# A recurrent attention kernel on one core: joint PV halves copied by bank, filler matmuls moved into the waits around Wo, the part copy in one instruction, and layer norm of the x rows one segment earlier

## The chip, the cores and the metric

The kernel runs on one core of one Trainium2 chip. The metric is device time in microseconds (us); a quoted time is the median of several executions. The engines are PE (TensorE), DVE (VectorE), ACT (ScalarE), POOL (GpSimd) and SP, which here only starts DMAs. The granted clock is the share of the full TensorE clock that the profile records as let through.

## The reference, cut to what matters

Part A is a transformer with a recurrent memory. It walks over 64 segments of 32 rows; 8 memory rows of each segment's output are the input of the next, so the segments form a chain. Part B, which follows, is a gated MLP and is not touched by the change.

```python
for s in range(n_seg):                       # 64 segments
    xs = x[:, s * seg_len:(s + 1) * seg_len, :]
    h = jnp.concatenate([mem, xs], axis=1)   # 8 memory rows + 32 rows
    q, k, v = h @ Wq, h @ Wk, h @ Wv         # 32 heads of 128 (written short)
    p = _softmax(jnp.where(mask, q @ k.T * scale, -1e9))
    o = einsum('bhte,hed->btd', p @ v, Wo)
    mem = o[:, :M, :]                        # M = 8: feeds the next segment
    outs.append(o[:, M:, :])
```

## The kernel before

A small emitter records every operation in program order with the tiles that it reads and writes, and derives semaphore waits. Each engine is given its own operations in program order, and in the traces they come in that order (PE from 502.66 to 507.24 us of before: PV, PV, Wo, WoX, mem_out, then the next Q/K). Two engines that read one PSUM bank are made to wait for each other.

The heads are handled in two halves `b` of 16. Names used below: **Q/K** are the 64 matmuls that project a segment (`QK`); **PV** is probabilities times V for one half; **Wo** is the output projection; **part copy** brings its result from PSUM to SBUF; **mem_out** makes the next memory rows of it. Work that no segment waits for is used as filler: **WoX** is the output projection of rows that were set aside, batched over four segments, and **V rows** (`gv`) and Q/K of x rows (`gx`) are projections of a later chunk of x.

```python
# end of a segment, before
ev = gv.pour(VXN[i16])          # V rows: 8 matmuls in most segments, 16 in two of 16, 0 in the last two
ev += gx.pour(16)               # Q/K of x rows, 16 matmuls
PV_half(s, 0)                   # writes columns 0:160 of banks 0, 1, 6, 7
cT_evac(0, 0, "act")            # banks 0 and 1
cT_evac(0, 1, "dve")            # banks 6 and 7
PV_half(s, 1)                   # the same columns again: must wait for the copies
cT_evac(1, 0, "act")
cT_evac(1, 1, "dve")
for f in ev: f()                # copies of finished V rows (ACT) and Q/K rows (DVE)
Wo(0); Wo(1)                    # 32 matmuls into bank OB
cTx_copy(s)
part_evac(s)                    # ACT 256 columns, then DVE 256 columns of the same bank
late = []
if rb > 0: WoX_mm(rb - 1, j4)   # 8 matmuls
if j4 == 2 and 3 <= rb + 2 < RB:
    ln_inplace(0)               # layer norm of 128 x rows: DVE, POOL, DVE
    xT(0, XB)                   # 4 PE transposes of them
    late.append(lambda: ring_copy(rb + 2, XB))
# ... the same with index 1 for i16 == 13 ...
mem_out(s)                      # 16 small matmuls, then ACT writes hT of segment s + 1
for f in late: f()
if rb > 0 and j4 == 3: WoX_evac(rb - 1)           # ACT: PSUM to SBUF
# ... cut ...
if j4 == 3: F_group(rb, XB); F_add(rb, XB)
if j4 == 3 and rb >= 1: WoX_scatter(rb - 1, WXB); h_done(rb - 1, WXB)   # PE, waits for WoX_evac
```

`j4` is the segment's index modulo 4, `i16` modulo 16, and `rb` counts blocks of four segments. The chunks of x rows are used up after 48 segments, so the last 16 segments have neither `gv` nor `gx`.

## Time and profile before

| | before |
|---|---|
| median | 1140.59 us (1138.38 to 1141.48) |
| the 64 segments, of the 1143.7 us span | 56.1 to 926.1 us |
| ordinary segment (start of Q/K to start of the next Q/K) | 12.42 us; 11.97 in the last 16 |
| every fourth segment (j4 = 2) and its follower | 15.05 and 14.8 us |

The page of the profile, lines of the span, of PE's busy time and of the chain that ended last (the last work, followed back step by step to what released it); the row PEclk shows 40 slices of the span, in tenths of the full TensorE clock.

```profile
span 1143.7 us, 41433 instructions
...
PE 947.0 (83%) x18997; PEld 468.6 (41%) x18997; DVE 504.7 (44%) x1123; ACT 483.1 (42%) x1095; POOL 108.0 (9%) x276
...
PEclk8799999999999999999999999989899879999999
...
PE 73%; ACT 12%; DVE 6%; issue 2%; SPq 2%; DMA 2%; POOL 1%; ACTq 0%
```

TensorE is the chain, but not all of it: the rest are waits for copies on ACT and DVE. The next view is the chain in order of time (start us, duration us, engine and line) through the end of an ordinary segment.

```profile
502.73 0.20 PE f_ps L546 x16
...
503.05 0.43 ACT f_cT L565
...
503.52 0.37 PE f_ps L546 x16
...
503.92 1.87 PE f_ps L576 x32
...
505.82 0.39 ACT f_part L587
...
506.23 0.43 DVE f_part L588
...
506.71 0.25 PE f_ps L594 x8
...
506.99 0.20 ACT f_hT L597
...
507.24 3.64 PE f_ps L436 x64
```

PV of half 0 (L546) has to be copied (L565) before half 1 may overwrite the banks, and Wo (L576) starts 1.19 us after the first PV. From Wo's end at 505.79 to the next Q/K (L436) it is 1.45 us: two copies one after the other, then half of mem_out (L594), then a small copy. The two halves of the part copy read one bank; this kernel's emitter makes the second reader wait for the first, and the trace shows it as ACT 0.39 and then DVE 0.43.

The same view at the end of a segment with j4 = 2:

```profile
531.50 0.61 DVE f_st L334
...
532.14 0.19 DVE f_mv L335
...
532.41 0.23 POOL f_rs L336
...
532.72 0.58 POOL f_rs L338
...
533.32 0.42 DVE f_xn L340
...
533.79 0.40 PE f_ps L346 x4
...
534.71 5.33 PE f_ps L436 x64
```

Here layer norm (L334 to L340) is on the chain, because the transposes (L346) wait for it and mem_out stands behind the transposes in PE's order. And the next Q/K take 5.33 us, not 3.64. The view by stretches (stretch, its length, then busy us of PE and so on; the figure 1.00 or 0.68 after POOL is the granted clock) shows why:

```profile
519.66:523.30 3.64, 3.64 (x81) 1.90 (x85) 1.08 (x3) 1.79 (x3) 0.00 (x0) 1.00 0.58 156
534.71:540.04 5.33, 5.33 (x82) 2.37 (x85) 1.08 (x3) 2.12 (x4) 0.00 (x0) 0.68 0.01 3
```

The waits, longest in total first (who <- for whom: us in total, times, longest), have this for the layer norm and for the PV copies:

```profile
PE f_ps L346 <- DVE f_xn L340: 56.6, 20, 5.8
...
PE f_ps L546 <- ACT f_cT L565: 35.1, 64, 0.6
```

### The profile page before, as it was taken

What the parts mean: (1) busy time and instruction counts of PE and PEld (TensorE: products, weight loads), DVE (VectorE), ACT (ScalarE), POOL (GpSimd) and SP (SyncE); (2) the same over time, 40 slices, a digit from 0 to 9 for tenths busy, and PEclk for the clock granted to TensorE, in tenths of its full rate; (3) what the DMA queues carried; (4) which work ended last, traced back from release to release, by engine and by line L of the source; (5) the groups of instructions that cost most, each with busy time, mean ns of one, the idle gap of its engine ahead of it and who ended that gap; (6) DMA issues with size and microseconds to landing.
All of it is one profiled execution on the core that took longest, in us unless ns stands there. A gap on an engine that the chain in (4) does not pass through costs nothing.

```text
span 1143.7 us, 41433 instructions
## 1 busy us (share of the span) xinstructions
PE 947.0 (83%) x18997; PEld 468.6 (41%) x18997; DVE 504.7 (44%) x1123; ACT 483.1 (42%) x1095; POOL 108.0 (9%) x276
## 2 busy tenths in 40 slices
PE   5588888878888888788888888878788857799998
PEld 5344444434444444344444444433333313334443
DVE  2144454444444545454545444444444335544343
ACT  2155544544454545454545454545454423520000
POOL 4000010010000001010001000100101001210000
PEclk8799999999999999999999999989899879999999
DMA  9931111111111212111111120201011036002201
GB/s 343 293 76 41 30 44 31 48 38 37 31 44 30 44 30 54 32 37 31 44 30 50 29 60 17 60 16 50 22 38 42 11 116 230 1 1 83 92 14 34
DMA packets 93492, 67.36 MB, mean 59 GB/s; under 512 B 54392, under 2 KB 78336, under 8 KB 93312
## 3 DMA queue, kind: packets, MB, share of 16 engines
q1 hardware_dynamic: 93312, 64.65, 18.9%
q8 instruction: 151, 2.47, 0.9%
q14 instruction: 29, 0.24, 0.1%
HBM read 39.46 MB, written 16.78 MB: 49 GB/s over the span
## 4 chain that ended last, share of the span: by engine, by line
PE 73%; ACT 12%; DVE 6%; issue 2%; SPq 2%; DMA 2%; POOL 1%; ACTq 0%
PE f_ps L436 22%; PE f_ps L576 11%; PE f_ps L952 9%; PE f_ps L530 7%; PE f_ps L380 5%; PE f_ps L546 3%; PE f_ps L496 3%; DVE f_part L588 2%; ACT f_cT L565 2%; ACT f_E_sb L489 2%; ACT f_part L587 2%; ACT f_R_sb L508 2%; PE f_ps L399 2%; PE f_ps L907 2%; PE f_ps L940 2%
## 5 line engine op out<-in xcount | busy, mean ns | idle before, releaser
L436 PE MATMUL f_ps<-f_arena,f_hT 128*32 128x512 bf16 x4096 | 255.5, 406 | 15.2 <-ACT f_hT L597 15.1
L443 ACT ACTIVATE f_Tst<-f_ps 128x512 bf16<-128x512 f32 x256 | 152.9, 597 | 142.8 <-PE f_ps L436 142.8
L436 PEld LDWEIGHTS f_ps<-f_arena,f_hT 128*32 128x32 bf16 x4096 | 111.3, 102 | 136.2 <-issue 29.3
L530 PE MATMUL f_ps<-f_arena,f_hT 128*32 128x512 bf16 x2048 | 143.6, 378 | 0.0
L576 PE MATMUL f_ps<-f_arena,f_cT 128*32 128x512 bf16 x2048 | 132.0, 403 | 0.0
L449 DVE STREAM_TRANSPOSE f_QT<-f_Tst 128x256 uint32<-128x256 uint32 x128 | 56.5, 442 | 156.7 <-ACT f_Tst L443 156.7
L952 PE MATMUL f_ps<-f_arena 128*128 128x512 bf16 x448 | 99.3, 379 | 3.0 <-DVE f_arena L957 2.4
L567 DVE TENSOR_SCALAR f_cT<-f_ps 128x320 bf16<-128x320 f32 x128 | 63.0, 492 | 70.6 <-PE f_ps L552 70.6
L565 ACT ACTIVATE f_cT<-f_ps 128x320 bf16<-128x320 f32 x128 | 56.0, 437 | 79.9 <-PE f_ps L552 79.9
L452 DVE STREAM_TRANSPOSE f_KT<-f_Tst 128x256 uint32<-128x256 uint32 x128 | 57.0, 445 | 63.4 <-ACT f_Tst L443 63.4
L346 PE MATMUL f_ps<-f_ident,f_xn 128*128 128x128 bf16 x144 | 16.1, 243 | 80.9 <-DVE f_xn L340 56.6
L546 PE MATMUL f_ps<-f_E_sb,f_V_sb 32*128 32x40 bf16 x2048 | 43.8, 179 | 46.9 <-ACT f_cT L565 35.1
L459 POOL COPY f_QT<-f_arena 128x256 bf16<-128x256 bf16 x64 | 29.9, 467 | 438.8 <-PE f_ps L481 438.7
L576 PEld LDWEIGHTS f_ps<-f_arena,f_cT 128*32 128x32 bf16 x2048 | 50.8, 100 | 50.1 <-issue 8.7
L380 PE MATMUL f_ps<-f_hTe,f_arena 128*128 128x128 bf16 x1024 | 69.6, 226 | 0.0
L380 PEld LDWEIGHTS f_ps<-f_hTe,f_arena 128*128 128x128 bf16 x1024 | 61.1, 102 | 20.4 <-issue 20.4
L588 DVE CAST f_part<-f_ps 128x256 bf16<-128x256 f32 x64 | 27.2, 425 | 91.6 <-ACT f_part L587 91.6
L952 PEld LDWEIGHTS f_ps<-f_arena 128*128 128x128 bf16 x448 | 43.5, 98 | 56.5 <-DVE f_arena L957 3.8
L516 DVE SCALAR_TENSOR_TENSOR f_E_sb<-f_R_sb,f_E_sb 128x160 bf16<-128x160 f32 x128 | 41.7, 326 | 54.6 <-ACT f_R_sb L512 54.6
L587 ACT ACTIVATE f_part<-f_ps 128x256 bf16<-128x256 f32 x64 | 24.6, 384 | 88.1 <-PE f_ps L576 88.1
L546 PEld LDWEIGHTS f_ps<-f_E_sb,f_V_sb 32*128 32x128 bf16 x2048 | 28.8, 91 | 68.9 <-ACT f_cT L565 42.3
L489 ACT ACTIVATE f_E_sb<-f_ps,f_shift 128x224 bf16<-128x224 f32 x128 | 56.9, 445 | 0.0
(96 smaller groups left out, 1171.5 us busy)
## 6 DMA issues: line engine op xcount, KB each, us to landing
wT_d<-f_wst SPq DMA_DIRECT2D x32, 256.0 KB, 2.3
f_arena<-wT_d SPq DMA_DIRECT2D x32, 256.0 KB, 5.8
f_arena<-in_A_Wq_dram SPq DMA_DIRECT2D x4, 1024.0 KB, 8.7
f_arena<-in_A_Wk_dram SPq DMA_DIRECT2D x4, 1024.0 KB, 13.6
f_arena<-in_A_Wv_dram SPq DMA_DIRECT2D x4, 1024.0 KB, 11.6
f_arena<-in_A_Wo_dram SPq DMA_DIRECT2D x4, 1024.0 KB, 13.8
vext_d<-f_Vs SPq DMA_DIRECT2D x32, 128.0 KB, 2.0
f_Vx<-vext_d SPq DMA_DIRECT2D x64, 64.0 KB, 2.5
```

What stands on the lines that cost most here:

```text
L380: pe(lambda e, h=h, dc=dc, hh=hh: e.matmul(ps[:, bank, hh * 128:(hh + 1) * 128], lhsT=ws[:, dc, h * DH:(h + 1) * DH], rhs=hTe[:, ck % 2, d ...
L436: pe(lambda e, dc=dc, c=c, rhs=rhs: e.matmul(ps[32 * c:32 * c + 32, bank, :], lhsT=hT[:, sl, dc, :], rhs=rhs, start=(dc == 0), stop=(dc == ...
L443: act(lambda e: e.activation(out=Tst[:, tb, :].rearrange("p (hp i r) -> p hp i r", i=32, r=2), in_=ps[:, bank, :].rearrange("p (hp r i) -> ...
L449: dve(lambda e: e.transpose(out=dst, in_=src), reads=[("T", tb)], writes=[("QT", b)])
L452: dve(lambda e: e.transpose(out=dst, in_=src), reads=[("T", tb)], writes=[("KT", b)])
L489: act(lambda e: e.activation(out=E_sb[:, b, :], in_=ps[:, bank, 0:224], func=ACT.Exp, scale=scale, bias=shift_sb[:, 0:1]), reads=[PB(bank) ...
L530: pe(lambda e, dc=dc, c=c, c0=c0: e.matmul(ps[32 * c:32 * c + 32, bank, :], lhsT=hT[:, sl, dc, :], rhs=w_v[:, dc, c0:c0 + 512], start=(dc ...
L546: pe(lambda e, q=q, c=c, g=g: e.matmul(ps[:, PVB[c], g * 40:(g + 1) * 40], lhsT=V_sb[q, b, g * 128:(g + 1) * 128], rhs=E_sb[q, b, g * 40:( ...
L565: act(lambda e: e.activation(out=dst, in_=src, func=ACT.Copy, scale=UNSC), reads=[PB(b0), PB(b0 + 1)], writes=[("cT", b, part_)])
L567: dve(lambda e: e.tensor_scalar(out=dst, in0=src, scalar1=UNSC, scalar2=None, op0=ALU.mult), reads=[PB(b0), PB(b0 + 1)], writes=[("cT", b, ...
L576: pe(lambda e, h=h, c=c: e.matmul(ps[32 * c:32 * c + 32, OB, :], lhsT=cTh[:, h, 8:40], rhs=w_o[:, h, :], start=(h < 4), stop=(h >= H - 4), ...
L952: pe(lambda e, fb=fb, sc=sc, bank=bank, tb=tb: e.matmul(ps[:, bank, 0:TB], lhsT=z2[:, sc, fb * 128:(fb + 1) * 128], rhs=wTb[tb % 2][:, :, ...
```

## The change

Four things at once. (1) PV's two halves write different columns of the banks, so they run together, and each copy takes one bank with both halves in it; Wo takes the heads bank by bank. (2) WoX moves into the wait for these copies, and the V rows move from in front of PV into the wait for the part copy. (3) The part copy is one ACT instruction. (4) Loads and layer norm of the x rows come one segment before their transposes.

```diff
@@ PV_half: the same banks, other columns for b = 1
-                    ps[:, PVB[c], g * 40:(g + 1) * 40], lhsT=..., rhs=...,
+                    ps[:, PVB[c], c0:c0 + 40], lhsT=..., rhs=...,      # c0 = 160 * b + 40 * g
@@ cT_evac: one bank, both halves
-        src = ps[:, b0:b0 + 2, 0:160]
-        dst = cT[:, b, 2 * part_:2 * part_ + 2, :]
+        src = ps[:, PVB[c], 0:320]
+        dst = cT[:, c, :]
@@ part_evac
-        act(... out=part[:, s % 4, 0:256], in_=ps[:, OB, 0:256] ...)
-        dve(... out=part[:, s % 4, 256:512], in_=ps[:, OB, 256:512] ...)
+        act(... out=part[:, s % 4, :], in_=ps[:, OB, :] ...)
@@ the segment (load_x: j4 == 1 became j4 == 0; load_xe: i16 == 12 became 11)
-        ev = gv.pour(VXN[i16])
-        ev += gx.pour(16)
+        ev = gx.pour(16)
         PV_half(s, 0)
-        cT_evac(0, 0, "act")
-        cT_evac(0, 1, "dve")
         PV_half(s, 1)
-        cT_evac(1, 0, "act")
-        cT_evac(1, 1, "dve")
+        cT_evac(0, "act")
+        cT_evac(2, "dve")
+        cT_evac(1, "act")
+        cT_evac(3, "dve")
         for f in ev:
             f()
-        Wo(0)
-        Wo(1)
+        if rb > 0:
+            WoX_mm(rb - 1, j4)
+        Wo((0, 2), True, False)
+        Wo((1, 3), False, True)
         cTx_copy(s)
         part_evac(s)
-        late = []
-        if rb > 0:
-            WoX_mm(rb - 1, j4)
+        if j4 == 1 and 3 <= rb + 2 < RB:
+            ln_inplace(0)
+        if i16 == 12 and 2 <= ck + 1 < NCK:
+            ln_inplace(1)
+        late = gv.pour(VXN[i16])
         if j4 == 2 and 3 <= rb + 2 < RB:
-            ln_inplace(0)
             xT(0, XB)
... cut: the same for index 1, and the head order of WoX and cTx ...
```

More of the change, by code (lines that the diff above doesn't have):

```diff
@@ L217, in fast_path @@
     R_sb = sb("R_sb", [128, 2, 160], F32)
-    cT = sb("cT", [128, 2, 4, 160], BF)
+    cT = sb("cT", [128, 4, 320], BF)
     part = sb("part", [128, 4, 512], BF)
@@ L545, in PV_half @@
                 q = slice(32 * c, 32 * c + 32)
-                pe(lambda e, q=q, c=c, g=g: e.matmul(
-                    ps[:, PVB[c], g * 40:(g + 1) * 40], lhsT=V_sb[q, b, g * 128:(g + 1) * 128], rhs=E_sb[q, b, g * 40:(g + 1) * 40],
+                c0 = 160 * b + 40 * g
+                pe(lambda e, q=q, c=c, g=g, c0=c0: e.matmul(
+                    ps[:, PVB[c], c0:c0 + 40], lhsT=V_sb[q, b, g * 128:(g + 1) * 128], rhs=E_sb[q, b, g * 40:(g + 1) * 40],
                     start=(g == 0), stop=False, skip_group_check=True, tile_position=(32 * c, 0)),
@@ L552, in PV_half @@
             pe(lambda e, q=q, c=c: e.matmul(
-                ps[:, PVB[c], 0:160].rearrange("p (g q) -> p g q", q=40)[:, :, 0:16], lhsT=Vx[q, xb, b, :],
+                ps[:, PVB[c], 160 * b:160 * b + 160].rearrange("p (g q) -> p g q", q=40)[:, :, 0:16], lhsT=Vx[q, xb, b, :],
                 rhs=E_sb[q, b, 160:224].rearrange("p (g q) -> p g q", q=16),
@@ L558, in fast_path, with cT_evac, Wo @@
     UNSC = 2.0 ** -64
-    def cT_evac(b, part_, eng):
-        b0 = 0 if part_ == 0 else 6
-        src = ps[:, b0:b0 + 2, 0:160]
-        dst = cT[:, b, 2 * part_:2 * part_ + 2, :]
+    def cT_evac(c, eng):
+        src = ps[:, PVB[c], 0:320]
+        dst = cT[:, c, :]
         if eng == "act":
-            act(lambda e: e.activation(out=dst, in_=src, func=ACT.Copy, scale=UNSC), reads=[PB(b0), PB(b0 + 1)], writes=[("cT", b, part_)])
+            act(lambda e: e.activation(out=dst, in_=src, func=ACT.Copy, scale=UNSC), reads=[PB(PVB[c])], writes=[("cT", c)])
         else:
             dve(lambda e: e.tensor_scalar(out=dst, in0=src, scalar1=UNSC, scalar2=None, op0=ALU.mult),
-                reads=[PB(b0), PB(b0 + 1)], writes=[("cT", b, part_)])
-    cTh = cT[:].rearrange("p b c (g q) -> p (b c g) q", q=40)
-    def Wo(b, lo=0, hi=16):
-        for hh in range(lo, hi):
-            h = 16 * b + hh
-            c = h % 4
-            pe(lambda e, h=h, c=c: e.matmul(ps[32 * c:32 * c + 32, OB, :], lhsT=cTh[:, h, 8:40], rhs=w_o[:, h, :],
-                                            start=(h < 4), stop=(h >= H - 4), tile_position=(0, 32 * c)),
-               reads=[("cT", b, hh // 8), ("Wo", h // 8)], writes=[PB(OB)])
+                reads=[PB(PVB[c])], writes=[("cT", c)])
+    cTh = cT[:].rearrange("p c (b g q) -> p (c b g) q", b=2, q=40)
+    def Wo(cs, first, last):
+        for k, c in enumerate(cs):
+            for bg in range(8):
+                b, g = bg // 4, bg % 4
+                h = 16 * b + 4 * c + g
+                i = 8 * c + bg
+                pe(lambda e, h=h, g=g, i=i, k=k, b=b: e.matmul(
+                    ps[32 * g:32 * g + 32, OB, :], lhsT=cTh[:, i, 8:40], rhs=w_o[:, h, :], start=(first and k == 0 and b == 0),
+                    stop=(last and k == len(cs) - 1 and b == 1), tile_position=(0, 32 * g)),
+                    reads=[("cT", c), ("Wo", h // 8)], writes=[PB(OB)])
     def cTx_copy(s):
@@ L582, in cTx_copy @@
         dst = cTx[:, (s // 4) % 2, :, 8 * j:8 * j + 8]
-        pool(lambda e: e.tensor_copy(out=dst, in_=cTh[:, :, 0:8]), reads=[("cT", b, p_) for b in range(2) for p_ in range(2)],
+        pool(lambda e: e.tensor_copy(out=dst, in_=cTh[:, :, 0:8]), reads=[("cT", c) for c in range(4)],
              writes=[("cTx", (s // 4) % 2)])
     def part_evac(s):
-        act(lambda e: e.activation(out=part[:, s % 4, 0:256], in_=ps[:, OB, 0:256], func=ACT.Copy), reads=[PB(OB)], writes=[("part", s % 4, 0)])
-        dve(lambda e: e.tensor_copy(out=part[:, s % 4, 256:512], in_=ps[:, OB, 256:512]), reads=[PB(OB)], writes=[("part", s % 4, 1)])
+        act(lambda e: e.activation(out=part[:, s % 4, :], in_=ps[:, OB, :], func=ACT.Copy), reads=[PB(OB)], writes=[("part", s % 4)])
     def mem_out(s):
@@ L595, in mem_out @@
                                                          rhs=G_sb[:, :], start=True, stop=True, skip_group_check=True, tile_position=(0, 32 * c)),
-                   reads=[("part", s % 4, dc // 2), "G"], writes=[PB(GB)])
+                   reads=[("part", s % 4), "G"], writes=[PB(GB)])
         act(lambda e: e.activation(out=hT[:, slot(s + 1), :, 0:M], in_=ps[:, GB, 0:DC * M].rearrange("p (dc c) -> p dc c", c=M), func=ACT.Copy),
@@ L604, in F_group @@
                                        tile_position=(0, 32 * j)),
-               reads=[("part", j, 0), ("part", j, 1), "F"], writes=[PB(bank)])
+               reads=[("part", j), "F"], writes=[PB(bank)])
     def F_add(rb, bank):
@@ L614, in WoX_mm @@
     def WoX_mm(rb, qr):
-        for hh in range(8):
-            h = 8 * qr + hh
-            c = h % 4
-            pe(lambda e, h=h, c=c: e.matmul(ps[32 * c:32 * c + 32, WXB, :], lhsT=cTx[:, rb % 2, h, :], rhs=w_o[:, h, :],
-                                            start=(h < 4), stop=(h >= H - 4), tile_position=(0, 32 * c)),
+        for bg in range(8):
+            b, g = bg // 4, bg % 4
+            h = 16 * b + 4 * qr + g
+            pe(lambda e, h=h, g=g, i=8 * qr + bg: e.matmul(ps[32 * g:32 * g + 32, WXB, :], lhsT=cTx[:, rb % 2, i, :], rhs=w_o[:, h, :],
+                                                           start=(i < 4), stop=(i >= H - 4), tile_position=(0, 32 * g)),
                reads=[("cTx", rb % 2), ("Wo", h // 8)], writes=[PB(WXB)])
@@ L738, in fast_path @@
             wT_piece(s // 2)
-        if j4 == 1 and 3 <= rb + 2 < RB:
+        if j4 == 0 and 3 <= rb + 2 < RB:
             load_x(rb + 2, 0)
-        if i16 == 12 and 2 <= ck + 1 < NCK:
+        if i16 == 11 and 2 <= ck + 1 < NCK:
             load_xe(ck + 1, 1)
@@ L788, in fast_path @@
         if i16 == 13 and 2 <= ck + 1 < NCK:
-            ln_inplace(1)
             xT(1, XB)
```

## The prediction

> **What bounds it now.** The recurrence over 64 segments takes 870 of the 1143.7 us span (timeline: first segment at 56.1 us, last ends at 926.1); the 217 us after it do not change. Inside a segment TensorE works in program order and is the chain: the chain of waits gives PE 73%, ACT 12%, DVE 6%. Starts of the segments' Q/K matmuls (PE timeline) give 12.42 us for an ordinary segment, 11.97 us in the last 16 (no filler), but 15.05 us for every fourth, followed by 14.8 us.
>
> **The long segments.** There the timeline shows PE idle 2.75 us before the transposes L346: layer norm of the x rows (0.69 + 0.18 on DVE, 0.22 + 0.57 on POOL, 0.41 on DVE, with hops) starts only after DVE's half of the part copy, and the transposes stand ahead of mem_out in PE's order. Excess 15.05 - 12.42 = 2.63 us, 15 times. In 13 of them the next Q/K matmuls then take 5.3 us (once 6.1, once 4.8), not 3.64; the windows view gives a clock of 0.68 there against 1.00. [...]
>
> **Costing of the change** (chain of waits, ordinary segment):
> 1. Layer norm one segment earlier runs while DVE has nothing urgent. Saves 15 x 2.63 = 39 us, less about 0.3 us each because the transposes (0.4 us) now follow the V rows in the part wait: -35 us.
> 2. With that idle gone, the slow Q/K stretches go: 13 x 1.69 = 22, counted as -20 us.
> 3. PV: now PV0, copies 0.43, PV1, first Wo matmul 1.19 us after PV0's start. Together: PV about 0.5, one copy 0.49 of each bank pair, second pair hidden behind Wo's first half; WoX's 0.43 us fills the copy wait. About 1.0 us: 64 x 0.19 = -12 us.
> 4. Part copy: now ACT 0.39, then DVE 0.43 after it, mem_out in two parts, 1.45 us from Wo's end to the next Q/K. One 512-wide ACT copy (0.59, as L406) and all of mem_out: about 1.20. 64 x 0.25 = -16 us.
> 5. V rows (L399, 8 matmuls 0.43 us) leave the stretch before PV, where TensorE was full, for the part wait, where they fit: 36 x 0.43; in 6 segments with 16 of them 0.2 no longer fits: -19 us.
> 6. Added: the V copy on ACT (0.59) now stands ahead of WoX_evac in the 8 segments where both occur, and the scatter waits for it: +5 us.
> 7. The last 16 segments have six Wo at 3.56 us instead of 1.87 (slow clock). WoX in the copy wait thickens that stretch: perhaps -3 us.
>
> Sum about -100 us; nearly all is on the chain. I take 1044 us, 80% range 1028 to 1064. Faster by over 2%: 0.96; within 2%: 0.03; slower: 0.01.
>
> **What would show it.** Idle before L346 from layer norm falls from 56.6 us to the start-up's part; Q/K at 3.64 us throughout; PE waits "L546 <- ACT cT" (35 us) vanish; segments near 11.5 us, every fourth about 0.4 to 0.9 longer; Wo's end to Q/K about 1.2 us; scatter waits (9 us) grow by about 5.
>
> **What would make it wrong.** The clock: the wait positions move, the last 16 segments lose WoX from their part wait, and new slow stretches of 1.7 us each could appear, or all vanish (10 us more). The switch between row-tiled PV and column-tiled WoX might cost, or Wo might wait for the DVE copy longer than thought. Layer norm on DVE could delay the next Q transpose.

The sum: -35 - 20 - 12 - 16 - 19 + 5 - 3 = -100 us. The 1.69 us of item 2 is what the trace of before shows, 5.33 - 3.64 us.

## The result, and the profile after

| | before | after |
|---|---|---|
| median | 1140.59 us | 1034.06 us (1033.13 to 1034.27) |
| ratio | | 0.9067 (0.9051 to 0.9083) |
| profiled span, mean clock | 1143.7 us, 0.954 | 1032.3 us, 0.983 |
| ordinary segment | 12.42; 11.97 in the last 16 | 11.64; 11.62 in the last 16 |
| j4 = 2, j4 = 3 | 15.05, 14.8 | 11.64, 12.84 |

A ratio is the mean time of one kernel's runs over that of the other's in the same rounds, so it is not quite the ratio of the medians. Executions over 1.5% slower than the fastest of the same kernel are left out of the means. All outputs are right. The profiled execution of before was a slowish one (1145.67 us); so the spans differ by 111.4 us and the medians by 106.5.

The page of after, the same lines:

```profile
span 1032.3 us, 41294 instructions
...
PE 899.6 (87%) x18986; PEld 443.2 (43%) x18997; DVE 471.5 (46%) x1059; ACT 489.8 (47%) x1095; POOL 108.0 (10%) x276
...
PEclk9889999999999999999999999999999979999999
...
PE 79%; ACT 12%; DVE 3%; SPq 2%; issue 2%; DMA 2%; POOL 0%; ACTq 0%
```

PE's busy time fell by 47 us although it does the same matmuls: at a lower clock the same matmuls are busy for longer (64 Q/K for 5.33 us at a mean clock of 0.68, 3.64 us at 1.00), and PV halves that run together overlap. (The Q/K matmuls are busy for 255.5 us before and 233.4 after, Wo for 132.0 and 122.3, PV's 2048 on V rows for 43.8 and 30.2.) The chain through the end of an ordinary segment of after (L547 and L553 are PV, L621 WoX, L579 Wo, L591 the part copy, L597 mem_out):

```profile
457.46 0.20 PE f_ps L547 x16
...
457.70 0.12 PE f_ps L547 x16
...
457.86 0.55 PE f_ps L621 x8
458.40 1.94 PE f_ps L579 x32
...
460.37 0.60 ACT f_part L591
...
461.02 0.32 PE f_ps L597 x16
...
461.36 0.21 ACT f_hT L600
...
461.61 3.64 PE f_ps L436 x64
```

The chain shows the first PV piece late, because the matmuls before it still count; PE's timeline has the starts:

```profile
457.39 0.27 PE L547 MATMUL f_ps<-f_E_sb,f_V_sb 32*128 32x40 bf16 x16
...
458.40 1.91 PE L579 MATMUL f_ps<-f_arena,f_cT 128*32 128x512 bf16 x32
```

Wo now starts 1.02 us after the first PV (1.19 before, from 502.66 to 503.85 in the same view), and from Wo's end to the next Q/K it is 1.27 us (1.45 before). The wait of the transposes for layer norm is down to the start-up's part, and PE no longer waits for a PV copy before PV (the scatter's wait for WoX_evac grew from 9.1 to 13.3 us in all):

```profile
PE f_ps L346 <- DVE f_xn L340: 15.2, 5, 5.7
```

One thing got worse. In segments with j4 = 3 the chain of after has two ACT copies in a row:

```profile
484.64 0.20 ACT f_hT L600
484.83 0.49 ACT f_Vs L406
485.32 0.50 ACT f_partx L626
...
485.86 0.40 PE f_ps L631 x4
486.26 3.45 PE f_ps L436 x64
```

The copy of V rows (L406), now issued late, stands ahead of WoX_evac (L626), for which the scatter (L631) and behind it Q/K wait. These segments take 12.84 us, those with j4 = 3 and no V-row copy 12.35 us.

The 111.4 us of the profiles, sorted with the segment starts of both:

| term | predicted | measured | how |
|---|---|---|---|
| layer norm's wait | -35 | -39 | 13 x 2.6 (two of them slightly more) and 2 x 2.2 |
| slow Q/K behind it | -20 | -22 | the 13 Q/K over 3.64 us, summed |
| PV together, part copy in one | -28 | -22 | 64 x 0.35, the saving of a segment without V rows |
| V rows out of the stretch before PV | -19 | -21 | 36 x 0.43 and 6 x 0.86 |
| V copy ahead of WoX_evac | +5 | +4 | 8 x 0.50 |
| slow Wo in the last 16 segments | -3 | -10 | six Wo over 1.87 us, summed |
| rest (start, the end of part A) | 0 | about -1 | the difference to 111.4 |

### The profile page after: what moved, and what is told of

Read it like the earlier page. It is cut to its first block, busy times and chain, and to the rows that moved or that the text cites. A ratio compares the mean times of both kernels' runs of the same rounds, so it can differ in the third digit from the quotient of the medians.

```text
span 1032.3 us, 41294 instructions
## 1 busy us (share of the span) xinstructions
PE 899.6 (87%) x18986; PEld 443.2 (43%) x18997; DVE 471.5 (46%) x1059; ACT 489.8 (47%) x1095; POOL 108.0 (10%) x276
## 4 chain that ended last, share of the span: by engine, by line
PE 79%; ACT 12%; DVE 3%; SPq 2%; issue 2%; DMA 2%; POOL 0%; ACTq 0%
PE f_ps L436 22%; PE f_ps L579 12%; PE f_ps L956 9%; PE f_ps L530 7%; PE f_ps L380 6%; PE f_ps L621 3%; ACT f_part L591 3%; PE f_ps L496 3%; ACT f_E_sb L489 3%; ACT f_R_sb L508 2%; PE f_ps L911 2%; PE f_ps L944 2%; PE f_ps L547 2%; PE f_ps L597 2%; PE f_ps L878 2%
## 5 line engine op out<-in xcount | busy, mean ns | idle before, releaser
L436 PE MATMUL f_ps<-f_arena,f_hT 128*32 128x512 bf16 x4096 | 233.4, 380 | 15.7 <-ACT f_hT L600 15.6
L436 PEld LDWEIGHTS f_ps<-f_arena,f_hT 128*32 128x32 bf16 x4096 | 105.2, 97 | 120.7 <-ACT f_hT L600 20.5
L530 PE MATMUL f_ps<-f_arena,f_hT 128*32 128x512 bf16 x2048 | 143.6, 378 | 0.0
L579 PE MATMUL f_ps<-f_arena,f_cT 128*32 128x512 bf16 x2048 | 122.3, 380 | 2.2 <-ACT f_cT L566 2.2
L591 ACT ACTIVATE f_part<-f_ps 128x512 bf16<-128x512 f32 x64 | 38.2, 597 | 108.0 <-PE f_ps L579 108.0
L579 PEld LDWEIGHTS f_ps<-f_arena,f_cT 128*32 128x32 bf16 x2048 | 48.8, 96 | 74.0 <-ACT f_cT L566 32.3
L568 DVE TENSOR_SCALAR f_cT<-f_ps 128x320 bf16<-128x320 f32 x128 | 56.9, 487 | 33.0 <-PE f_ps L553 33.0
L566 ACT ACTIVATE f_cT<-f_ps 128x320 bf16<-128x320 f32 x128 | 49.0, 434 | 37.1 <-PE f_ps L553 37.1
L512 ACT ACTIVATE f_R_sb<-f_R_sb,f_rbias 128x160 f32<-128x160 f32 x128 | 54.0, 422 | 2.1
L508 ACT ACTIVATE f_R_sb<-f_ps 128x160 f32<-128x160 f32 x128 | 39.0, 304 | 29.8 <-PE f_ps L501 25.0
L961 DVE TENSOR_TENSOR f_arena<-f_ps,f_arena 128x512 f32<-128x512 f32 x28 | 19.4, 692 | 70.6 <-PE f_ps L956 70.6
```

Of the source, the lines that this page charges most:

```text
L436: pe(lambda e, dc=dc, c=c, rhs=rhs: e.matmul(ps[32 * c:32 * c + 32, bank, :], lhsT=hT[:, sl, dc, :], rhs=rhs, start=(dc == 0), stop=(dc == ...
L508: act(lambda e: e.activation(out=R_sb[:, b, :], in_=ps[:, bank, 224:384], func=ACT.Ln, scale=LNS), reads=[PB(bank)], writes=[("R", b)])
L530: pe(lambda e, dc=dc, c=c, c0=c0: e.matmul(ps[32 * c:32 * c + 32, bank, :], lhsT=hT[:, sl, dc, :], rhs=w_v[:, dc, c0:c0 + 512], start=(dc ...
L568: dve(lambda e: e.tensor_scalar(out=dst, in0=src, scalar1=UNSC, scalar2=None, op0=ALU.mult), reads=[PB(PVB[c])], writes=[("cT", c)])
L579: pe(lambda e, h=h, g=g, i=i, k=k, b=b: e.matmul(ps[32 * g:32 * g + 32, OB, :], lhsT=cTh[:, i, 8:40], rhs=w_o[:, h, :], start=(first and k ...
L591: act(lambda e: e.activation(out=part[:, s % 4, :], in_=ps[:, OB, :], func=ACT.Copy), reads=[PB(OB)], writes=[("part", s % 4)])
```

## The experiments

Nine kernels, each against the kernel before on the same chip, timed in rounds with it. Names that begin with b are the kernel before with one thing added; those with a are the kernel after with one thing undone or altered.

### b_ln_only: only layer norm moved

```diff
-        if j4 == 1 and 3 <= rb + 2 < RB:
+        if j4 == 0 and 3 <= rb + 2 < RB:
             load_x(rb + 2, 0)
@@ (and load_xe at i16 == 11; behind part_evac:)
+        if j4 == 1 and 3 <= rb + 2 < RB:
+            ln_inplace(0)
+        if i16 == 12 and 2 <= ck + 1 < NCK:
+            ln_inplace(1)
@@
         if j4 == 2 and 3 <= rb + 2 < RB:
-            ln_inplace(0)
             xT(0, XB)
```

> The kernel before with only the loads and the layer norm of the x rows moved up one segment. Theory: the 15 waits of 2.63 us go, and with them the slow clock of the Q/K matmuls behind them (12 to 13 times 1.69 us), about -61 us: 1079 us; Q/K after the transposes at 3.64 us. The slow Wo stretches (3.56 us) of the last 16 segments stay, since their cause is another. Rival: the clock falls because of the other bubbles of a segment and only happens to land on those Q/K matmuls; then the slow stretches reappear elsewhere and only the 39 us go: 1101 us.

Measured: 1083.29 us, ratio 0.9504 (0.9456 to 0.9551), 57 us less than before. All j4 = 2 segments take 12.42 us like their neighbours (11.99 and 11.97 where there are no V rows), and no Q/K behind them is slow. Five slow Wo stay in the last 16 segments. The rival's 1101 us is refuted: with the wait gone, the slow Q/K were gone too (13 in before's profile, none here but the first segment's). WoX (0.43 us) and the transposes fit into the 0.9 us of the old part copy.

### b_fill: useless work inside the wait

This asks for the cause of the slow clock alone: the wait stays, and only its idleness is taken away. (The extra results are overwritten.)

```diff
         if j4 == 2 and 3 <= rb + 2 < RB:
             ln_inplace(0)
+            for _ in range(10):
+                for c in range(4):
+                    pe(lambda e, c=c: e.matmul(ps[32 * c:32 * c + 32, XB, :], lhsT=ident[:, 0:32], rhs=w_o[:, c, :], ...))
             xT(0, XB)
```

> The kernel before with 40 useless matmuls (128x512 on a 128x32 weight tile, results overwritten by the transposes) placed in front of the transposes of the x rows, about 2.2 us of TensorE work inside the 2.75 us wait for layer norm. Layer norm and its wait stay. Theory (the clock falls because TensorE is idle there): the long segments stay at 15.05 us, but the Q/K matmuls after them take 3.64 us again: 13 x 1.69 = -22 us, 1118 us; slow Wo stretches of the last 16 segments may stay. Rival (the slow clock has nothing to do with idleness there, or only fewer instructions on the chain help): 1140 us, Q/K still at 5.3 us.

Measured: 1120.62 us, ratio 0.981 (0.9777 to 0.9843), which is clear of 1 but unclear at the 2% line. The kernel does 600 matmuls more and is 20 us faster. Timeline of PE in this kernel (L788 are the useless matmuls; in brackets, idle time before and what ended it):

```profile
518.56 2.33 PE L788 MATMUL f_ps<-f_arena,f_ident 128*32 128x512 bf16 x40
521.48 0.40 PE L346 MATMUL f_ps<-f_ident,f_xn 128*128 128x128 bf16 x4 [0.59 <-DVE f_xn L340]
...
522.40 3.64 PE L436 MATMUL f_ps<-f_arena,f_hT 128*32 128x512 bf16 x64 [0.33 <-ACT f_hT L597]
```

The transposes come as late as before (the segment still takes 15.05 us), but all 13 Q/K that were slow in before are at 3.64 us. So it is TensorE's idleness in this wait that brings the slow clock here: 13 slow Q/K with it, none with 2.33 us of matmuls in it. An estimate of the cost from the trace of before: half speed from 535.63 to 539.03 us (the second stretch below) loses 3.41 / 2 = 1.7 us; 5.33 - 3.64 = 1.69 agrees.

The clock records of the traces show more. In all eleven profiles the granted clock is 1.00 or 0.50 (0.68 above is a mean over a stretch), and the recorded changes lie whole multiples of 3.41 us apart (all 49 changes in before, all 9 in after). Points at such a multiple from a recorded change are called grid points below. Here are two stretches of before from one grid point to the next, around the slow Q/K at 534.71, and then the least busy one around the wait of b_fill:

```profile
532.21:535.62 3.41, 1.50 (x40) 0.87 (x44) 0.53 (x2) 0.58 (x2) 0.79 (x2) 1.00 0.00 0
535.63:539.03 3.40, 3.40 (x40) 1.31 (x36) 0.89 (x2) 1.20 (x2) 0.00 (x0) 0.50 0.02 5
...
520.28:523.68 3.40, 2.48 (x56) 1.16 (x52) 0.41 (x1) 0.76 (x3) 0.61 (x2) 1.00 0.02 5
```

From the second segment on, the eleven profiles have 2456 such stretches at full clock. All 29 with PE busy for less than 1.5 us were followed by half speed, none of the 2376 with more than 2.0 us was; of the 51 in between 37 were. (In before: 13 of 13, none of 257, 8 of 18; in after: 1 of 1, none of 267, none of 8.) These are counts of what these profiles hold; what decides in between is not shown.

### b_pv_only: only PV together and copied by bank

The edit is the first two blocks of the change's diff, with Wo's order; WoX, V rows, part copy and layer norm stay as in before.

> The kernel before with only both PV halves together, the copies by bank and Wo in that order; WoX, the V rows, the part copy and layer norm as before. Theory: the copy of the first two banks, not the filling of its wait, sets Wo's start: about 1.0 us after PV0 instead of 1.19, 64 x 0.19, 1128 us. Rival: the gain needs WoX in the wait: 1140 us.

Measured: 1123.25 us, ratio 0.9843 (0.9808 to 0.9877), clear of 1. An ordinary segment takes 12.25 us (12.42), so 64 x 0.17 = 11 us come from the copies alone, as the theory has it. Of the other 6 us about 4 are clock, by the profiles: this one has ten slow Q/K and five slow Wo (20 and 7 us lost), before has 13 and six (22 and 10). Since these move between executions, they are not credited to the edit; the remaining 2 us are not explained.

### b_vrows_only: only the V rows moved

```diff
-        ev = gv.pour(VXN[i16])
-        ev += gx.pour(16)
+        ev = gx.pour(16)
@@
-        late = []
+        late = gv.pour(VXN[i16])
         if rb > 0:
             WoX_mm(rb - 1, j4)
```

> The kernel before with only the V rows moved from before PV to the wait after Wo (beside WoX). Theory: 36 x 0.43 and some more in the 6 segments with 16 rows, less 8 x 0.5 because the V copy then stands ahead of WoX_evac on ACT: about -15 us, 1125 us. Rival: the place before PV was a wait too (for the last exponentials and the V copy), so nothing comes of it: 1140 us.

Measured: 1123.31 us, ratio 0.985 (0.9793 to 0.9908), formally unclear at the 2% line. The segments speak plainly: 11.99 us instead of 12.42 with 8 V-row matmuls, 12.24 instead of 12.85 with 16. The cost of the V copy ahead of WoX_evac shows here too: a j4 = 3 segment with a V copy and no slow Q/K is 1.2 us longer than an ordinary one, and 0.7 in b_ln_only. This profile also has only ten slow Q/K, so a part of its gain is clock. The stretch in front of PV was then full (8 V-row matmuls fewer there, 0.43 us less), and the wait behind Wo had room for WoX and 8 V-row matmuls.

### a_ln_back: after with layer norm in its old segment

The reverse of b_ln_only, on the kernel after.

> The kernel after with the loads and the layer norm back in their old segment. If the parts simply add, this is 61 us slower than after: 1095 us. Theory: DVE no longer has half of the part copy and starts layer norm right after its Q/K-of-x copy, so the wait before the transposes is only about 1.25 us: +19 us with a full clock, up to +40 with slow stretches: 1053 to 1074 us.

Measured: 1051.31 us, ratio 0.9218 (0.9185 to 0.9251). On top of the other parts, the layer norm move is worth only 17 us, though alone on before it was worth 57. DVE, free of its half of the part copy, starts layer norm about 0.95 us before Wo's end (528.08 against 529.03 in one segment) and not 0.8 us after it (531.42 against 530.61 in before); the long segments are 12.71 us, 1.07 longer than their neighbours and not 2.6. And behind that shorter wait the clock stays full: no Q/K is slow in this profile but the first segment's, where before had 13 of 15. (Two of its stretches of 3.41 us had PE busy for 1.95 and 1.97 us, where both outcomes occur, so in these two the full clock may be luck.) The parts do not add: cutting the wait's cost from 2.6 to 1.07 us a segment already took away the slow stretch of 1.69 us behind it, and taking away the rest brought no more clock.

### a_wox_back: after with WoX behind Wo again

```diff
-        if rb > 0:
-            WoX_mm(rb - 1, j4)
         Wo((0, 2), True, False)
@@
         late = gv.pour(VXN[i16])
+        if rb > 0:
+            WoX_mm(rb - 1, j4)
```

> The kernel after with WoX back behind Wo, so that it shares the part wait with the V rows and nothing fills the wait for the PV copies. Theory: the copies set Wo's start, so filling saves nothing there; but V rows and WoX together (0.86 us) are longer than the part wait (0.68): about 0.2 us in 36 segments, +7 us. In the last 16 segments the stretch before Wo gets thinner and the slow Wo stretches (3.56 us instead of 1.87) come back, up to +10 us: 1041 to 1051 us. Rival: the filling itself is worth its 0.43 us in 60 segments: 1060 us, and the clock of the last 16 segments stays full.

Measured: 1045.34 us, ratio 0.9173 (0.9155 to 0.919), 11 us slower than after. An ordinary segment is still 11.64 us: WoX in the PV wait saves nothing by itself there, because the copies set Wo's start, and WoX with 8 V rows still fits behind Wo. So "0.2 us in 36 segments" was wrong. What costs are 14 segments in which transposes or 16 V-row matmuls come on top, at 0.42 us each (6 us), and four slow Wo in the last 16 segments (6 us). Timeline of one of them:

```profile
774.84 3.56 PE L579 MATMUL f_ps<-f_arena,f_cT 128*32 128x512 bf16 x32 [0.54 <-ACT f_cT L566]
```

What differs is how busy TensorE is in the 3.41 us in front of Wo. The view by stretches (first figure behind the length: PE busy us) for the one ahead of a slow Wo in before:

```profile
890.59:894.00 3.41, 1.98 (x67) 0.79 (x56) 1.90 (x6) 2.52 (x7) 0.47 (x1) 1.00 0.02 5
```

ahead of this slow Wo in a_wox_back:

```profile
771.43:774.84 3.41, 1.97 (x88) 0.78 (x77) 1.99 (x7) 2.73 (x8) 0.47 (x1) 1.00 0.02 5
```

and ahead of a Wo in the last 16 segments of after:

```profile
775.38:778.79 3.41, 2.52 (x97) 0.90 (x84) 1.99 (x7) 2.73 (x8) 0.47 (x1) 1.00 0.30 101
```

With WoX in that stretch, PE is busy for 2.52 us and not 1.98. Over all eleven profiles the split is complete:

| WoX behind PV | slow Wo in the last 16 segments |
|---|---|
| no: before, b_ln_only, b_pv_only, b_vrows_only, b_fill, a_wox_back | 6, 5, 5, 6, 7, 4 |
| yes: after, a_ln_back, a_part_split, a_evac_order, a_evac_early | 0, 0, 0, 0, 0 |

Why four to seven of the 16 and not all? In the first row PE is busy for 1.98 us (once 1.89) ahead of every one of the 96 Wo, slow or not, so this alone does not decide. What differs in the traces is where a Wo falls between the grid points: all 33 slow Wo start between 0.6 us before and 0.2 us after a grid point, and of the other 63 only one does. (In before, the six slow ones start 0.02 to 0.44 us before one, and the other ten at least 0.5 us away.)

### a_part_split: after with the part copy in two halves

The edit restores the two lines of part_evac, and mem_out's waits by halves.

> The kernel after with the part copy in two halves again, ACT then DVE. Theory: 0.15 us more from Wo's end to the next Q/K (0.39 + 0.43 and hops, then half of mem_out, against 0.61 and all of it), 64 times: +10 us, 1044 us. Rival: with the V rows in that wait the split costs nothing: 1034 us.

Measured: 1045.71 us, ratio 0.9175 (0.916 to 0.9191), 11.6 us slower than after; the segments take 11.82 us instead of 11.64. 64 x 0.18 = 11.5. One copy of 512 columns (0.60 us, L591 of after) beats two of 256 that the emitter does not let overlap (0.39 and 0.43 us in before).

### a_evac_order: WoX_evac ahead of the late copies

```diff
         mem_out(s)
-        for f in late:
-            f()
         if rb > 0 and j4 == 3:
             WoX_evac(rb - 1)
+        for f in late:
+            f()
```

> The kernel after with one change of order: WoX_evac stands before the late copies (of V rows) on ACT. Theory: takes back the 0.5 us that every fourth segment lost in 8 cases: -4 us, 1030 us. Rival: that segment is longer for another reason, no change.

Measured: 1031.16 us, ratio 0.9047 (0.9032 to 0.9062). Every j4 = 3 segment now takes 12.35 us; the eight at 12.84 are gone. The 4 us of the prediction's item 6 are recovered, less a little (2.9 us by the medians). The intervals of the two ratios overlap, so the gain rests on the segments, not on the times.

### a_evac_early: WoX_evac behind the PV copies

WoX is finished before Wo starts, so its copy need not wait until mem_out.

```diff
         Wo((1, 3), False, True)
+        if rb > 0 and j4 == 3:
+            WoX_evac(rb - 1)
         cTx_copy(s)
@@
-        if rb > 0 and j4 == 3:
-            WoX_evac(rb - 1)
```

> The kernel after with WoX_evac issued on ACT right behind the PV copies, where ACT is idle for 1.7 us; WoX is done by then. Theory: the scatter no longer waits; every fourth segment is about 0.35 us longer than the others instead of 1.22 (8 times) and 0.72 (7 times): -9 us, 1025 us, the best so far. Rival: the copy delays the part copy on ACT and loses as much.

Measured: 1020.13 us (1019.79 to 1021.56), ratio 0.8956 (0.8942 to 0.897): the fastest kernel here, 14 us under after. The chain through the end of a j4 = 3 segment of this kernel:

```profile
475.18 0.61 ACT f_part L591
...
475.83 0.27 PE f_ps L597 x16
476.09 0.23 PE f_ps L606 x4
476.33 0.22 PE f_ps L631 x4
476.54 3.51 PE f_ps L436 x64
```

The scatter (L631) runs straight behind mem_out and F_group (L606), inside the time in which Q/K wait for hT anyway. The segment takes 11.64 us, like any other; the theory left it 0.35 us longer, so it undersold this.

## Why the prediction was right, point by point

The prediction said 1044 us with 1028 to 1064, and 1034.06 was measured. Every term had the sign that it was given, with these sizes; that the sum came so close is in part luck, since item 7 was 7 us too small and items 3 and 4 together 6 us too large:

- Item 1 (layer norm): 39 us, not 35. The 0.3 us set aside for the transposes behind the V rows were not lost: V rows and transposes (0.43 + 0.33 on the chain) end about when the part copy does, and only the two segments with transposes and 16 V-row matmuls are longer, by 0.42 us. The item is right for this set of edits in this order; a_ln_back shows that the same move is worth 17 us when it is the last one.
- Item 2 (slow Q/K): 22 us, of which 20 were counted. b_fill shows the cause directly. That 13 of 15 waits were followed by a slow Q/K belongs in part to where this kernel's waits fall: four of its segments last 54.7 us, nearly 16 times 3.41, so 11 of the 13 waits began at about the same place, 2.2 to 3.3 us behind a grid point. In b_pv_only and b_vrows_only the same 15 waits brought ten slow Q/K each.
- Items 3 and 4 (PV and part copy): 22 us, not 28. PV together gave 0.17 us a segment against 0.19 assumed (b_pv_only), the part copy 0.18 against 0.25 (a_part_split): from Wo's end to the next Q/K it is 1.27 us and not 1.20.
- Item 3 also said that WoX "fills the copy wait". It does, but the fill as such is worth nothing in an ordinary segment (a_wox_back); its worth is room behind Wo, 6 us, and the clock of the last 16 segments.
- Item 5 (V rows): 21 us, not 19, since 16 V-row matmuls fit too where no transposes come with them.
- Item 6 (V copy ahead of WoX_evac): 4 us of loss against 5 predicted, and shown by a_evac_order.
- Item 7 is the term that was mis-sized. "Perhaps -3 us" was about -10: all slow Wo went and not some.
- Of the signs, "every fourth about 0.4 to 0.9 longer" failed: segments with the transposes are not longer (but for the two of item 1), those with the scatter are longer by 0.7 to 1.2 us.
- Of what could have made it wrong, the switch between row-tiled PV and column-tiled WoX cost little. Eight WoX matmuls right behind PV take 0.55 us on the chain of after, and 0.43 behind the V rows in a_wox_back, as do the eight V-row matmuls behind Wo there; so by this estimate the switch costs at most about 0.12 us.

The prediction summed its terms to about -100 and settled on -97. The terms as measured sum to -110 in the two profiles; the medians differ by 106.5, because the profiled execution of before was 5 us slower than its median. So most of what was missing is item 7 and item 1, partly offset by items 3 and 4. That after has no slow stretch behind its first segment (the granted clock is 1.00 from 58.5 us to 823.0 us, which is past the last segment's Wo) is shown for the profiled execution alone; the narrow spread of its times (1033.13 to 1034.27, against 1136 to 1145 for before over all rounds) fits it.

## What to carry to other kernels

When TensorE, which takes its work in program order, waits for a side job, look first at where the side job starts and not at how long it takes: with layer norm issued one segment earlier, the segments with transposes take 11.64 us here like their neighbours (but for two, 12.06). Count an idle TensorE twice where the trace shows a lower clock after it (here 2.6 us of wait, and 1.69 us of slow Q/K behind it), and look for thin stretches as well as for long waits: here filler removed the slow clock behind a long wait (b_fill) and behind a stretch that had no gap over 0.63 us (WoX ahead of Wo: PE busy for 2.52 us of 3.41 and not 1.98). Ask also whether a slow stretch depends on where it falls (the same 15 waits brought 13 slow Q/K in before and ten in b_pv_only); then another edit may move it. When you move filler, follow its copies too: the engine that empties it took them in order as well (ACT: L406 at 484.83, then L626 at 485.32), and a copy that lands ahead of a critical one gives back part of the gain (4 us here).
